# Squares of the first unit split by part over ScalarE and VectorE, one square of products moved to VectorE in two units, and a longer assumed delay for K~ read back from memory

## The chip, the cores and the metric

The kernel runs on one core of a Trainium2 chip. The metric is the device time of one execution in microseconds (us), given as the median of several runs. The core has five engines that run beside each other and meet at semaphores: TensorE (PE in the profile, with its weight loads apart as PEld), VectorE (DVE), ScalarE (ACT), GpSimd (POOL) and SyncE (SP). Transfers to and from memory go by DMA queues, whose issues stand on SP, POOL or ACT.

## The reference: what is computed

A gated linear attention with a complex decay feeds a two-layer block with a squared ReLU between the layers. Batch 4, 8 heads, sequence 768, head size 48; the block is 384 wide and 2048 deep, over 3072 tokens.

```python
mag = np.sqrt(a_re * a_re + a_im * a_im)
scale = np.minimum(mag, 0.999) / (mag + 1e-06)
a_re_n, a_im_n = (a_re * scale, a_im * scale)
for t in range(S):
    ar, ai = (a_re_n[:, :, t, :, None], a_im_n[:, :, t, :, None])
    new_re = ar * S_re - ai * S_im
    new_im = ar * S_im + ai * S_re
    kv = np.einsum('bhd,bhe->bhde', k[:, :, t], v[:, :, t])
    S_re, S_im = (new_re + kv, new_im)
    y[:, :, t] = np.einsum('bhd,bhde->bhe', q[:, :, t], S_re)
# x = y by tokens, heads side by side: (3072, 384)
h = x @ w_in
r = np.maximum(h, 0.0)
out = (r * r) @ w_out
```

## The kernel before

The work is cut into 8 units: one half sequence (384 steps) of one batch entry each, numbered n = 0 to 7. Within a unit the 8 heads stand in two groups of four, z = 0 and z = 1. Each unit has three parts.

The **chain** makes the running products of the decay. On 128 partitions with three steps each (c = 0, 1, 2) it squares the decays, adds the squares, gets 1/mag by logarithm, exponential and a correction step, limits the magnitude, multiplies the three steps of a partition (the "inner" products), takes the reciprocal of the squared magnitude of these products, and turns the last product of each partition by TensorE so that a scan along the free dimension can finish the products over all 384 steps.

```python
def square(z):
    u["fa", z] = wk.tile([C, 2, HH, W, D], F32, name=f"fa{z}", tag=f"fa{z}")
    u["fb", z] = wk.tile([C, 2, HH, W, D], F32, name=f"fb{z}", tag=f"fb{z}")
    act.activation(out=whole(u["fa", z]), in_=whole(u["a", z]), func=AF.Square,
                   accum_out=sums[:, n, z:z + 1])      # sums: watched for overflow

def add_squares(z):
    f0, f1, g0, _ = parts(z)
    dve.tensor_tensor(out=g0, in0=f0, in1=f1, op=ALU.add)
# ...
D1, A1 = dve_cost(NEL), act_cost(NEL)                  # NEL = 4 * 3 * 48 = 576
one("sq", "ACT", act_cost(2 * NEL) + 90,
    lambda z: [("ld", n, "a", z, 1), ("ap", n - 1, z), ("carry", n - 1, 0)], square)
one("m2", "DVE", D1, lambda z: [("sq",)], add_squares)
one("ln", "ACT", A1, ...)                              # log of mag squared
one("ex", "ACT", A1, ...)                              # 1/mag
one("s2", "ACT", A1, ...)                              # its square
one("r1", "DVE", D1, ...); one("r2", "DVE", D1, ...)   # correction step
one("n1", "ACT", A1, ...); one("n2", "ACT", A1, ...)
one("l1", "DVE", D1, ...); one("l2", "DVE", dve_cost(2 * NEL), ...)   # limit
# "in10" ... "in23": the inner products, 16 instructions of VectorE per unit
one("me", "ACT", A1 + 90, lambda z: [("r2",)], lambda z: measure(2 + z, parts(z)[3]))
one("e1", "ACT", ..., lambda z: ends(z, 0))            # copy the last products
one("iq", "ACT", act_cost(2 * NEL), lambda z: [(f"in{W - 1}3",)],
    lambda z: act.activation(out=whole(u["fa", z]), in_=whole(u["a", z]),
                             func=AF.Square))
one("ia", "DVE", D1, lambda z: [("iq",)], add_squares)
one("il", "ACT", A1, ...); one("ie", "ACT", A1, ...)
one("i1", "DVE", D1, ...); one("i2", "DVE", D1, ...)
# ("tot", n, j) on PE turns the last products; ("et", n, j) copies them from PSUM into e
# the scan: 11 products on VectorE over e ("times", "plus")
```

The **pair steps** take two heads at a time: transposes of Q and K ("tq"), scores ("sa"), the outer products of K and V ("kv"), the mix into y ("mix"), and y's way into xT by DMA. "kv" reads K~ in another order of its rows than the chain leaves it in, so K~ goes through memory: "rows" writes it and "KC" reads it back, both as DMA on GpSimd's queue.

```python
for name, lag, deps in (
        ("rows", 4800 if whole_z else 3800, keys + [...]),
        ("KC", 5200 if whole_z else 4200,        # whole_z: units 2 to 7
         [("rows", n, z, pairs[0])] + [...])):
    add((name, n, z, pairs[0]), "POOL", 750, deps,
        lambda z=z, i=pairs[0], name=name: rows(z, i, name == "KC"),
        rank=-100, lag=lag)
```

The **dense steps** are the two layers: 48 products "h" (128x384) and 48 products "o" per unit.

All steps are first collected with an engine, a cost, a lag, a rank and what they depend on. A list scheduler in the kernel's source (`lay_out`) then places them on a model clock, and the steps are emitted in that order. So costs and lags in the source are assumptions: they change no duration on the chip, only the fixed order of the instructions on each engine.

```python
def step(key, engine, cost, rank, deps, fn, lag=None, bank=None, until=None):
    steps[key] = (engine, cost, LAG.get(engine, 0) if lag is None else lag, rank,
                  deps, fn, bank, until)
# lay_out: done[key] = t + cost + lag; a step is ready when all it depends on is done;
# among those ready at nearly the same time the lowest rank is taken
for _, key in lay_out():
    emit(steps[key][5])
```

## Time and profile before

Three runs took 755.68, 757.92 and 759.61 us. The profiled execution took 756.12 us by the same measure and spans 754.3 us in the trace.

| engine | busy us | share of the span | instructions |
|---|---|---|---|
| TensorE, matmul | 708.0 | 94% | 3578 |
| TensorE, weight load | 475.0 | 63% | 3578 |
| VectorE | 504.6 | 67% | 1200 |
| ScalarE | 412.6 | 55% | 764 |
| GpSimd | 113.7 | 15% | 165 |

| stretch, us | PE busy | DVE busy | ACT busy | what runs |
|---|---|---|---|---|
| 0 to 24.4 | 0.00 | 14.95 | 12.11 | unit 0's chain up to the inner products |
| 24.4 to 34.7 | 3.80 | 7.49 | 8.79 | squares of the products, reciprocal, first scan step |
| 34.7 to 47.5 | 10.43 | 12.18 | 8.67 | the scan; PE runs filler products |
| 60 to 85 | 23.16 | 23.36 | 12.54 | pair steps of unit 0, weights converted |
| 85 to 112 | 26.82 | 25.73 | 23.87 | first layer of unit 0 |
| 112 to 145 | 33.00 | 30.09 | 16.02 | second layer of unit 0, chain of unit 1 |
| 300 to 400 | 98.24 | 79.24 | 68.17 | units 3 and 4 |
| 400 to 500 | 99.15 | 87.30 | 68.25 | units 5 and 6 |

How to read it: the second table shows the stages apart, because the shares over the whole span hide that in the first 24.4 us PE does nothing at all, while in the middle it is busy nearly all the time. "Busy" counts instructions in execution; a row of the timeline gives the start, the duration, the engine, the source line, the operation with output and input, and in brackets the idle time just before it with what ended it.

### The profile page before, as it was taken

What the parts mean: (1) busy time and instruction counts of PE and PEld (TensorE: products, weight loads), DVE (VectorE), ACT (ScalarE), POOL (GpSimd) and SP (SyncE); (2) the same over time, 40 slices, a digit from 0 to 9 for tenths busy, and PEclk for the clock granted to TensorE, in tenths of its full rate; (3) what the DMA queues carried; (4) which work ended last, traced back from release to release, by engine and by line L of the source; (5) the groups of instructions that cost most, each with busy time, mean ns of one, the idle gap of its engine ahead of it and who ended that gap; (6) DMA issues with size and microseconds to landing.
All of it is one profiled execution on the core that took longest, in us unless ns stands there. A gap on an engine that the chain in (4) does not pass through costs nothing.

```text
span 754.3 us, 10015 instructions
## 1 busy us (share of the span) xinstructions
PE 708.0 (94%) x3578; PEld 475.0 (63%) x3578; DVE 504.6 (67%) x1200; ACT 412.6 (55%) x764; POOL 113.7 (15%) x165
## 2 busy tenths in 40 slices
PE   0389899999999999999999999999999999999996
PEld 0258555686667766766776676677677555555553
DVE  5899998977698897679689889958953561000000
ACT  6646495256938657762886578776155204402500
POOL 5003100052013013011301211210021430000000
PEclk9999999999999999999999999999999999999999
DMA  9617760054026114222602432340050990000000
GB/s 283 177 41 214 246 211 12 21 168 127 1 72 197 29 50 165 82 59 83 187 18 48 168 111 48 117 152 24 24 189 8 302 306 34 0 23 10 1 10 24
DMA packets 39195, 76.25 MB, mean 101 GB/s; under 512 B 10880, under 2 KB 25312, under 8 KB 39136
## 3 DMA queue, kind: packets, MB, share of 16 engines
q0 software_dynamic: 14336, 53.88, 22.8%
q1 hardware_dynamic: 24672, 21.49, 9.3%
q8 instruction: 30, 0.49, 0.3%
q14 instruction: 29, 0.24, 0.1%
q10 hardware_dynamic: 128, 0.15, 0.1%
HBM read 56.62 MB, written 14.16 MB: 94 GB/s over the span
## 4 chain that ended last, share of the span: by engine, by line
PE 85%; DMA 5%; DVE 4%; ACT 2%; issue 1%; POOL 0%; ACTq 0%; POOLq 0%
PE o L1428 33%; PE h L1411 30%; PE sa L1280 5%; PE tq L1267 4%; DMA KC<-rows 4%; PE kv L1294 4%; PE P L1151 2%; PE ypair L1319 2%; PE ypair L1324 1%; DMA xT<-yt 1%; PE tot L953 1%; PE bk L953 1%; PE y L1319 1%; PE y L1324 1%; PE busy L1068 1%
## 5 line engine op out<-in xcount | busy, mean ns | idle before, releaser
L1411 PE MATMUL h<-xT,w 128*128 128x384 f32 x768 | 256.7, 487 | 2.2 <-DMA xT<-yt 2.2
L1428 PE MATMUL o<-w,g 128*128 128x384 f32 x768 | 255.3, 487 | 0.0
L1411 PEld LDWEIGHTS h<-xT,w 128*128 128x128 f32 x768 | 142.3, 190 | 93.6 <-issue 3.7
L1428 PEld LDWEIGHTS o<-w,g 128*128 128x128 f32 x768 | 142.9, 190 | 91.9 <-issue 0.2
L1418 ACT ACTIVATE g<-h 128x384 f32<-128x384 f32 x128 | 62.3, 487 | 90.2 <-PE h L1411 89.9
L1272 ACT COPY QKT<-tq 96x512 f32<-96x512 f32 x96 | 77.0, 867 | 36.2 <-PE tq L1267 35.7
L1433 ACT COPY ot<-o 128x384 f32<-128x384 f32 x24 | 11.5, 478 | 116.6 <-PE o L1428 116.5
L1421 ACT ACTIVATE g<-g 128x384 f32<-128x384 f32 x128 | 65.8, 522 | 2.9
L1267 PE MATMUL tq<-ident,QK 128*96 128x128 f32 x384 | 51.7, 273 | 1.2 <-DVE QK L1157 1.2
L1280 PE MATMUL sa<-QKT 96*128 96x128 f32 x384 | 52.4, 279 | 0.1
L1280 PEld LDWEIGHTS sa<-QKT 96*128 96x128 f32 x384 | 48.1, 192 | 6.1 <-issue 0.8
L1018 DVE TENSOR_TENSOR fa<-e 128x192 f32<-128x192 f32 (+4 forms) x144 | 48.1, 371 | 5.3 <-ACT e L989 3.1
L1267 PEld LDWEIGHTS tq<-ident,QK 128*96 128x96 f32 x384 | 42.9, 126 | 11.7 <-issue 7.7
L1286 DVE TENSOR_TENSOR A<-sa,mask 128x384 f32<-128x384 f32 x64 | 35.1, 553 | 21.0 <-PE sa L1280 20.0
L824 DVE TENSOR_TENSOR fb<-fa 128x576 f32<-128x576 f32 x32 | 24.1, 755 | 28.7 <-ACT fa L923 17.9
L953 PE MATMUL tot<-ident,last 128*128 128x128 f32 x72 | 12.5, 296 | 30.3 <-ACT last L878 24.4
L832 DVE SCALAR_TENSOR_TENSOR fb<-fb 128x576 f32<-128x576 f32 x48 | 35.1, 753 | 7.6 <-ACT fb L827 7.1
L827 ACT ACTIVATE fa<-fb 128x576 f32<-128x576 f32 x48 | 30.9, 676 | 13.6 <-DVE fb L824 11.3
L1025 DVE TENSOR_TENSOR e<-fa,fa 128x96 f32<-128x96 f32 (+6 forms) x160 | 35.7, 283 | 2.6
L1168 POOL DMA_DIRECT2D rows<-QK x20 | 12.6, 629 | 163.9 <-DVE QK L1157 162.9
L1294 PE MATMUL kv<-v,KC 128*96 128x48 f32 x320 | 31.4, 246 | 3.5 <-DMA KC<-rows 3.5
L1294 PEld LDWEIGHTS kv<-v,KC 128*96 128x96 f32 x320 | 30.4, 165 | 6.8 <-ACT g L1418 2.3
(122 smaller groups left out, 854.2 us busy)
## 6 DMA issues: line engine op xcount, KB each, us to landing
rows<-QK POOLq DMA_DIRECT2D x12, 576.0 KB, 3.6
raw<-in_moe_w_in_dram POOLq DMA_DIRECT2D x16, 384.0 KB, 7.8
look<-in_moe_w_in_dram POOLq DMA_DIRECT2D x16, 384.0 KB, 4.7
look<-in_moe_w_out_dram POOLq DMA_DIRECT2D x16, 384.0 KB, 4.5
raw<-in_moe_w_out_dram SPq DMA_DIRECT2D x13, 384.0 KB, 5.0
out_dram<-ot SPq DMA_DIRECT2D x24, 192.0 KB, 1.9
v<-in_v_dram POOLq DMA_DIRECT2D x18, 192.0 KB, 4.4
a<-in_a_re_dram POOLq DMA_DIRECT2D x12, 288.0 KB, 3.4
```

The source lines that it names most:

```text
L832: dve.scalar_tensor_tensor(out=f[dst[-1]], in0=f[2] if i == 0 else f[dst[0]], scalar=scalar, in1=f[by], op0=ALU.add if i else ALU.mult, op ...
L1018: dve.tensor_tensor(out=t, in0=x(e), in1=y(e)[:, j].unsqueeze(1) .to_broadcast(shape), op=ALU.mult)
L1025: dve.tensor_tensor(out=dst(u["e"])[:, r], in0=temp(0)[:, r], in1=temp(1)[:, 1 - r], op=ALU.add if r else ALU.subtract)
L1267: nc.tensor.transpose(ps[:, 2 * j + h], src, ident)
L1272: act.copy(out=u["T", i].rearrange("r z (p c) -> r c z p", c=W)[:, c], in_=u["tq", i, c])
L1280: nc.tensor.matmul(sa[:, j], lhsT=T[:, 2 + h, ts(j, C)], rhs=T[:, h, ts(j, C)], start=True, stop=True)
L1286: dve.tensor_tensor(out=u["A", i][:, h], in0=u["sa", i, h], in1=mask3, op=ALU.mult)
L1294: nc.tensor.matmul(ps[:, j, h], lhsT=u["KC", hh // HH][:, j, hh % HH], rhs=u["v"][:, j, hh], start=True, stop=True)
L1411: nc.tensor.matmul(u["h", f], lhsT=w1[:, f, m], rhs=u["xT"][:, m], start=(m == 0), stop=(m == NM - 1))
L1418: act.activation(out=t, in_=u["h", f], func=AF.Relu)
L1421: act.activation(out=u["g", f], in_=u["g", f], func=AF.Square)
L1428: nc.tensor.matmul(u["o", c], lhsT=u["g", f][:, ts(c, C)], rhs=w2[:, f], start=(f == 0), stop=(f == NF - 1))
```

## The change

The change has four parts and a small fifth. Its aim is a shorter way to TensorE's first work, and an order of TensorE's instructions that does not meet the transfer of K~ before it has landed.

1. Unit 0's squares of the decays: the square over both parts (1152 elements a partition, with a sum over the elements) is split. ScalarE squares the real part (576) as soon as that part has landed, VectorE squares the imaginary part by a multiplication with itself. The sum for the overflow watch is taken later, by a copy of the added squares with a sum ("ms"). The assumed lags of the four loads are set anew.
2. Units 0 and 1, group z = 1: the square of the inner products ("iq") is done by VectorE instead of ScalarE.
3. The assumed lag of "KC" in units 2 to 7 goes from 5200 to 7000.
4. `minus`, a negated identity, is made by ScalarE later, as a step of its own before the products that use it.
5. `LATER`, a rank, goes from 150 to 155, so that the ranks of the few postponed steps keep their place behind the steps that were added.

```diff
-    act.mul(out=minus, in_=ident, mul=-1.0)
...
-                        lag=(3300 + 2500 * z if name == "a" else 8000) if n == 0 else 6000)
+                        lag=(3100 + 1100 * z + 300 * j if name == "a" else 8000)
+                        if n == 0 else 6000)
...
+            elif r == 0:
+                act.activation(out=parts(z)[0], in_=flat(u["a", z][:, 0]), func=AF.Square)
+            else:
+                a = flat(u["a", z][:, 1])
+                dve.tensor_tensor(out=parts(z)[1], in0=a, in1=a, op=ALU.mult)
...
+        if n == 0:
+            one("sq", "ACT", A1, lambda z: [("ld", n, "a", z, 0)], lambda z: square(z, 0))
+            one("sqi", "DVE", D1, lambda z: [("ld", n, "a", z, 1), ("sq",)],
+                lambda z: square(z, 1))
+            one("ms", "ACT", A1 + 90, lambda z: [("m2",), ("me",)],
+                lambda z: measure(z, parts(z)[2], AF.Copy), rank=900)
+            add(("minus",), "ACT", 190, [("me", 0, 1)],
+                lambda: act.mul(out=minus, in_=ident, mul=-1.0), rank=910)
+        else:
+            one("sq", "ACT", act_cost(2 * NEL) + 90, ..., square)
+        one("m2", "DVE", D1, lambda z: [("sq",), ("sqi",)], add_squares)
...
-        one("iq", "ACT", act_cost(2 * NEL), lambda z: [(f"in{W - 1}3",)], ...)
-        one("ia", "DVE", D1, lambda z: [("iq",)], add_squares)
+        def square_products(z):
+            a, fa = whole(u["a", z]), whole(u["fa", z])
+            if n < 2 and z:
+                dve.tensor_tensor(out=fa, in0=a, in1=a, op=ALU.mult)
+            else:
+                act.activation(out=fa, in_=a, func=AF.Square)
+        both(lambda z: add(("iq", n, z), *(("DVE", dve_cost(2 * NEL)) if n < 2 and z else
+                                           ("ACT", act_cost(2 * NEL))),
+                           [(f"in{W - 1}3", n, z)], lambda: square_products(z)))
+        one("ia", "DVE", D1, lambda z: [("iq",), ("ms",)], add_squares)
...
-        LATER = 150
+        LATER = 155
...
-                        ("KC", 5200 if whole_z else 4200,
+                        ("KC", 7000 if whole_z else 4200,
```

Because the order is made from the assumed costs and lags, the change also moves instructions that the diff does not name. TensorE's order is the same up to the pair steps of unit 3. From there the first "kv" of units 3, 4, 6 and 7 stands later or behind other products, and from there to the last units the order differs in many places; VectorE's order differs in the two squares, in the first scan steps of units 0 and 1, and in the later units where it follows TensorE's.

## The prediction

> **What bounds the kernel now.** I read the engine totals and the slices of the page first, then TensorE's waits, then the timeline where the two meet.

> ```profile
> PE 708.0 (94%) x3578; PEld 475.0 (63%) x3578; DVE 504.6 (67%) x1200; ACT 412.6 (55%) x764; POOL 113.7 (15%) x165
> ...
> PE   0389899999999999999999999999999999999996
> ```

> Each digit is a fortieth of the span, 18.9 us. TensorE is idle in the first and part of the second and third slice and then close to full. So there are two ways to shorten the kernel without taking work from TensorE: let it start earlier, and take away its waits later. The waits are few:

> ```profile
> PE tot L953 <- ACT last L878: 24.4, 1, 24.4
> PE tot L953 <- ACT last L880: 5.9, 2, 4.9
> PE kv L1294 <- DMA KC<-rows: 3.5, 4, 1.8
> PE bk L953 <- DVE e L1025: 2.2, 1, 2.2
> PE h L1411 <- DMA xT<-yt: 2.2, 2, 1.4
> ```

> The columns are total us, times, longest. The first, second and fourth line are unit 0's chain; the third is K~ read back. In the chain the last to be ready is nearly always VectorE (12.18 of 12.80 us busy from 34.7 to 47.5 us), so I look for VectorE's gaps before that:

> ```profile
> 9.40 0.76 DVE L824 TENSOR_TENSOR fb<-fa 128x576 f32<-128x576 f32 x1 [2.61 <-ACT fa L819]
> ...
> 12.34 0.76 DVE L832 SCALAR_TENSOR_TENSOR fb<-fb 128x576 f32<-128x576 f32 x1 [0.61 <-ACT fb L827]
> ...
> 25.81 0.76 DVE L824 TENSOR_TENSOR fb<-fa 128x576 f32<-128x576 f32 x1 [1.79 <-ACT fa L923]
> 27.71 0.76 DVE L824 TENSOR_TENSOR fb<-fa 128x576 f32<-128x576 f32 x1 [1.14 <-ACT fa L923]
> ```

> From 12.34 us to 24.0 us VectorE has no gap; then it waits 1.79 and 1.14 us for ScalarE's two squares of the products (1.16 us each). These gaps are what the second part of the change aims at. The waits for K~ in units 3, 4 and 6:

> ```profile
> 297.56 1.53 PE L1294 MATMUL kv<-v,KC 128*96 128x48 f32 x16 [0.36 <-DMA KC<-rows]
> 368.46 1.19 PE L1294 MATMUL kv<-v,KC 128*96 128x48 f32 x12 [1.76 <-DMA KC<-rows]
> 492.60 2.21 PE L1294 MATMUL kv<-v,KC 128*96 128x48 f32 x24 [0.85 <-DMA KC<-rows]
> ```

> Together 2.97 us; the fourth wait, 0.53 us, is in unit 0, whose lag is not changed.

> [...] 758 and 1354 ns. The new squares on VectorE are tensor_tensors of these sizes, so I take 0.76 and 1.36 us. [...] every ScalarE row of the first 30 us starts after the row that stands before it in the order. [...] For K~ of a whole group (576 KB) [...] here it is 5.7 us in the median and 8.0 at most, and the measurement decides. So the source's new 7000 is the more honest one.

> **The change, part by part.**

> *Unit 0's first squares.* Landing times in the DMA view (issue plus time to landing): real and imaginary part of group 0 at 0.81 + 3.0 = 3.8 and 1.30 + 3.3 = 4.6 us; of group 1 at 1.84 + 5.0 = 6.8 and 2.39 + 5.4 = 7.8. Removed from ScalarE: two squares of 1.15 and two accumulator reads of 0.19 us. Added: two squares of 0.68 us (as the other 576-element activations), and on VectorE two of 0.76 us. ScalarE's new order is square 0, square 1, logarithm 0. Square 1 waits for 6.8 and ends near 7.6, so logarithm 0 starts near 7.6, where it now starts at 6.82[...]. What counts is when VectorE can run without gaps, at the second group's correction step, now 12.34. After: imaginary squares on VectorE at 4.7 and 7.85, sums of squares at 5.5 and 8.6, ready by 9.4. ScalarE from 7.6 does three activations per group at 0.72 us each, six in all: the last starts at 7.6 + 5 x 0.72 = 11.2 and ends at 11.9. So VectorE's unbroken stretch begins near 11.9 instead of 12.34. **Gain 0.4 to 0.5 us.** The new sums ("ms", 0.67 + 0.19 us each) fall in ScalarE's idle 7.86 us before 23.79, and so does `minus` (0.29): free.

> *Unit 0's squares of products.* Now VectorE loses 1.79 + 1.14 + 0.1 = 3.0 us in gaps between 24.0 and 29.0. After: VectorE squares group 1 itself as soon as the inner products end (1.3 us start to start), then adds group 1's squares (0.7); in that time ScalarE, which copies the last products (0.93) and squares group 0 (1.16) from 0.3 us before the same moment, is done, and group 0's sum follows without a gap. The copies of the turned products from PSUM (two, 0.93 us) come next on ScalarE and end 2.6 us after the inner products; VectorE is then 2.7 us on. So almost no gap: 3.0 - 1.3 = **1.7 us gain**. That the order puts four more scan instructions before the reciprocal's correction steps only shifts work within a stretch in which VectorE is full.

> With 0.45 from the front this is 2.1 us earlier for the scan's end at 45.8 us, and for all that follows: from there to 80 us VectorE (23.36 of 25 us) and TensorE (23.16 of 25) feed each other, and the transfers in it start from results, so they move along. The weights land long before they are used.

> *Unit 1's squares of products.* The same edit, but the gaps there are 1.79 and 0.30 us, and after the sums the scan waits for the turned products: TensorE gets to turn them only at 127.83, between second-layer products. After: square 125.75, sums at 127.05 and 127.75, ended 128.5; the copies from PSUM on ScalarE still end near 129.3, and the scan starts at 129.35, where it starts now (129.34). Gaps removed 2.09, work added 1.3, new gap 0.8: **0.0 us**.

> *K~'s lag.* From the first transposes of the unit (which start when "rows" is issued) to the first "kv", TensorE's order holds, with "h" of three 1.94 us, "o" of four 2.58, transposes of eight 0.87, scores of six 1.48:

> | unit | landed after | TensorE work ahead, before | after |
> |---|---|---|---|
> | 3 | 11.0 us | 10.65 | 13.3 |
> | 4 | 12.2 us | 10.55 | 13.3 |
> | 6 | 11.3 us | 10.65 | 11.8 |

> (For unit 3: 3 x 0.87 + 3 x 1.94 + 1.48 + 0.74 = 10.65; the new order puts 0.74 + 1.94 more ahead.) All three waits are covered, unit 6 with 0.5 us to spare. TensorE is otherwise full there, so what it doesn't wait is gained: up to 2.97, I take **2.7 us**.

> *What is given back.* From unit 3 on TensorE's order is another one, and the mix after a late "kv" now has 1.94 us between them in which VectorE adds up to six small states (0.28 us each): enough, but with less room. I put 0.5 us for new small waits.

> Sum: 2.1 + 0.0 + 2.7 - 0.5 = 4.3 us; 757.92 - 4.3 = **753.6 us**, 0.6% less.

> **The rivals.**

> *The K~ wait only changes its name.* ScalarE is busy 12.14 of 12.50 us in the 12.5 us before unit 4's "kv", with copies of the transposes and the squared ReLU of "h". If the products put ahead of "kv" are "h", each brings 1.0 us of ScalarE work and PSUM room must come free: TensorE could wait for ScalarE instead. For it speaks that number; against it that the page shows no TensorE wait for ScalarE behind unit 0, and that 1.94 us of "h" brings only 1.0 of ScalarE. It would give back 1.5 to 3 us: 755 to 757.

> *The head's gain is lost at a transfer.* TensorE waits 0.53 us for K~ and 1.44 us for xT at the end of unit 0's pair steps; if a transfer there were held by traffic that does not move along (weights at 178 GB/s in 60 to 85), the 2.1 us would shrink. Against it: those transfers are issued when their data is ready. It would leave 1 us of the head: 754.7.

> *VectorE pays for unit 1.* From 85 to 112 us it is busy 25.73 of 27, and 1.3 us of work is added in unit 1; if the turned products come earlier than I think the gap of 0.8 is not there (gain 0.8), if VectorE is late the reverse: 753 to 755.

> **Range and chances.** The three runs before spread over 3.9 us, so a median may be off by 1 to 1.5 us; the reordered units I put at 1.5 to 2 us. That gives 750.0 to 757.2 for 8 in 10. A gain of over 2% (15 us) would need about all of TensorE's waits after the first one (5.9 + 3.5 + 2.2 + 2.2 and 2.0 in smaller ones = 15.8 us); a loss of over 2% would need new waits of 15 us in an order that only moves one group of products by 2 to 4 us. Faster by over 2%: 0.01, within 2%: 0.97, slower by over 2%: 0.02.

> **What would show it.** In the changed profile: logarithm 0 starting near 7.6 us; TensorE's first wait near 23.9 instead of 24.4; VectorE's gaps after 24 us under 0.3 us in sum; the scan's end near 43.7; first-layer products of unit 0 resuming near 83.1 instead of 85.19; no waits of "kv" for K~ in units 3, 4 and 6. The prediction is wrong if the scan's end moves by less than 1.5 us, if the 2.1 us are gone by 85 us, or if TensorE's waits behind 185 us stay at 3 us under another name.

## The result, and the profile after

The changed kernel took **749.55 us** in the median (748.03 to 750.53, four runs), the kernel before 757.66 (755.68 to 759.61, four runs): a ratio of 0.9891, 95% interval 0.9859 to 0.9923. The prediction was 753.6 with a range of 750.0 to 757.2, so the time fell below the range. In three later series, on three chips, the ratios were 0.9907 (0.988 to 0.9935), 0.9926 (0.9906 to 0.9946) and 0.9898 (0.9873 to 0.9923). In differences of means these are 6.9, 5.9 and 7.1 us; the working had summed to 4.3.

The page of the changed kernel, engine totals and TensorE's slices (now 18.7 us each):

```profile
PE 704.8 (94%) x3578; PEld 473.7 (63%) x3578; DVE 508.7 (68%) x1204; ACT 412.0 (55%) x764; POOL 114.8 (15%) x165
...
PE   0379899999999999999999999999999999999996
```

TensorE does the same 3578 products in 3.2 us less busy time, which is a first hint that something other than waits has changed: equal products took less time. VectorE has its four added instructions.

TensorE's waits in the changed kernel (total us, times, longest):

```profile
PE tot L979 <- ACT last L886: 23.9, 1, 23.9
PE tot L979 <- ACT last L888: 5.6, 2, 5.4
PE kv L1320 <- DMA KC<-rows: 2.2, 1, 2.2
PE h L1437 <- DMA xT<-yt: 1.8, 2, 1.3
PE tq L1293 <- DVE QK L1183: 1.7, 1, 1.7
PE bk L979 <- DVE e L1051: 1.7, 1, 1.7
```

The first wait is 0.5 us shorter. "kv" waits for K~ once instead of four times, and the one that is left is in unit 0 and has grown from 0.53 to 2.24 us. From 200 us to 740 us the list of waits is empty. Line numbers are higher by 26 in this part of the source.

VectorE's timeline in the changed kernel, at the same places as in the prediction:

```profile
5.83 0.76 DVE L832 TENSOR_TENSOR fb<-fa 128x576 f32<-128x576 f32 x1
...
9.80 0.76 DVE L840 SCALAR_TENSOR_TENSOR fb<-fb 128x576 f32<-128x576 f32 x1 [0.20 <-ACT fb L835]
...
11.81 0.76 DVE L840 SCALAR_TENSOR_TENSOR fb<-fb 128x576 f32<-128x576 f32 x1 [0.45 <-ACT fb L835]
...
23.52 1.36 DVE L943 TENSOR_TENSOR fa<-a 128x1152 f32<-128x1152 f32 x1
24.98 1.43 DVE L832 TENSOR_TENSOR fb<-fa 128x576 f32<-128x576 f32 x2
26.52 0.92 DVE L1044 TENSOR_TENSOR fa<-e 128x192 f32<-128x192 f32 x2
```

A row without a bracket had no idle time before it. The second group's correction step starts at 11.81 instead of 12.34 us; from there VectorE runs through, its own square of the products (1.36 us) included, and the gaps of 1.79 and 1.14 us are gone. On ScalarE the first logarithm starts where the working put it, near 7.6:

```profile
7.08 0.68 ACT L825 ACTIVATE fa<-a 128x576 f32<-128x576 f32 x1 [2.23 <-DMA a<-in_a_re_dram]
7.67 0.67 ACT L835 ACTIVATE fa<-fb 128x576 f32<-128x576 f32 x1
```

Its input, the added squares of group 0 (the first row of VectorE's timeline), is ready at 6.59 us. The logarithm still starts 1.1 us later, behind group 1's square, which stands ahead of it in ScalarE's order and waits 2.23 us for its load.

The scan's last instruction (the second of L1051 over 279 elements, L1025 before) ends at 43.50 instead of 45.78 us. TensorE's timeline in the changed kernel where the head of the kernel (all that stands ahead of unit 1's first layer, up to about 185 us) comes to its transfers:

```profile
75.92 1.22 PE L1320 MATMUL kv<-v,KC 128*96 128x48 f32 x12 [2.24 <-DMA KC<-rows]
...
83.75 27.33 PE L1437 MATMUL h<-xT,w 128*128 128x384 f32 x84 [1.31 <-DMA xT<-yt]
```

Of the 2.3 us gained at the scan's end 1.44 us are left where the first layer resumes (83.75 against 85.19): the longer wait for K~ took the rest in this execution.

| point, us | before | after | gain so far |
|---|---|---|---|
| scan's last instruction ends | 45.78 | 43.50 | 2.28 |
| unit 0's first layer resumes | 85.19 | 83.75 | 1.44 |
| unit 1's first layer resumes | 184.78 | 182.98 | 1.80 |
| last product of TensorE ends | 748.22 | 742.77 | 5.45 |

The last two rows differ by 563.44 us before and 559.79 after. So this pair of executions puts 3.65 us into the part behind 185 us and 1.8 into the head. The medians of the later series are farther apart than that, and what is missing had to be looked for in executions, not in one profile.

### The profile page after: what moved, and what is told of

Its sections match the earlier page's. It is cut to its first block, busy times and chain, and to the rows that moved or that the text cites. A ratio compares the mean times of both kernels' runs of the same rounds, so it can differ in the third digit from the quotient of the medians.

```text
span 748.8 us, 10017 instructions
## 1 busy us (share of the span) xinstructions
PE 704.8 (94%) x3578; PEld 473.7 (63%) x3578; DVE 508.7 (68%) x1204; ACT 412.0 (55%) x764; POOL 114.8 (15%) x165
## 4 chain that ended last, share of the span: by engine, by line
PE 89%; DMA 3%; SPq 3%; DVE 2%; issue 1%; ACT 1%; POOL 0%; ACTq 0%; POOLq 0%
PE o L1454 33%; PE h L1437 32%; PE sa L1306 6%; PE tq L1293 5%; PE kv L1320 3%; SPq L783 2%; PE ypair L1345 2%; PE P L1177 2%; PE ypair L1350 1%; DMA xT<-yt 1%; PE tot L979 1%; DMA v<-in_v_dram 1%; PE bk L979 1%; DMA KC<-rows 1%; PE y L1345 1%
## 5 line engine op out<-in xcount | busy, mean ns | idle before, releaser
L979 PE MATMUL tot<-ident,last 128*128 128x128 f32 x72 | 12.3, 296 | 29.5 <-ACT last L886 23.9
L832 DVE TENSOR_TENSOR fb<-fa 128x576 f32<-128x576 f32 x32 | 24.0, 755 | 20.1 <-ACT fa L945 15.4
L1051 DVE TENSOR_TENSOR e<-fa,fa 128x96 f32<-128x96 f32 (+6 forms) x160 | 35.4, 283 | 2.6
L783 POOL DMA_DIRECT2D v<-in_v_dram x18 | 15.9, 888 | 115.3 <-PE y L1350 75.8
```

Of the source, the lines that this page charges most:

```text
L1051: dve.tensor_tensor(out=dst(u["e"])[:, r], in0=temp(0)[:, r], in1=temp(1)[:, 1 - r], op=ALU.add if r else ALU.subtract)
```

## The theories, and the experiments

**The working's own theory**: the gain is the sum of its steps, each wait being worth its length. **Rivals**: a part of the sum is mis-sized (the K~ step worth more, or the head worth less because a transfer eats it); or, called **theory D** in the expectations, a TensorE wait of 1 to 2 us has a price beside its length, because TensorE runs at half its clock for some microseconds afterwards (3.4 us in the kernel before, from 46.72 to 50.13 us). Each expectation says in its own words what else it sets against what.

The differences below are of means, against the kernel before run in the same series on the same chip; the medians of the kernel before were 754.69, 754.71, 755.26 and 755.54 in the four series. The ratio, with its 95% interval, is an estimate of its own and not the quotient of these means; the two differ by up to 0.8 us (fetch_late: 4.9 us by the means, 4.1 by the ratio). Where the text says "either way" it means twice the standard error of a difference of means.

| kernel | median us | runs | less than before, us | ratio (95%) |
|---|---|---|---|---|
| after_again | 748.35 | 6 | 6.85 | 0.9907 (0.988 to 0.9935) |
| kc_only | 752.35 | 22 | 2.67 | 0.996 (0.9947 to 0.9974) |
| no_kc | 750.47 | 13 | 3.96 | 0.9941 (0.9918 to 0.9963) |
| iq_only | 752.41 | 22 | 2.47 | 0.9972 (0.9956 to 0.9989) |
| fill_all | 755.14 | 14 | 0.03 | 0.9997 (0.9984 to 1.0011) |
| fewer_fill | 749.83 | 6 | 4.95 | 0.9941 (0.9924 to 0.9958) |
| fetch_late | 750.57 | 6 | 4.93 | 0.9945 (0.9924 to 0.9966) |
| iq_u0 | 748.98 | 6 | 5.75 | 0.9933 (0.9914 to 0.9952) |
| after_third | 749.45 | 6 | 5.89 | 0.9926 (0.9906 to 0.9946) |
| late_fill | 749.76 | 6 | 5.91 | 0.9931 (0.9912 to 0.9951) |
| fill_head | 754.34 | 14 | 1.09 | 0.9988 (0.9969 to 1.0006) |
| no_iq | 751.68 | 22 | 3.68 | 0.9956 (0.9944 to 0.9968) |
| more_before | 753.16 | 22 | 1.99 | 0.9972 (0.9958 to 0.9986) |
| fewer_before | 753.83 | 22 | 1.39 | 0.998 (0.9964 to 0.9996) |
| more_after | 748.68 | 6 | 6.75 | 0.9905 (0.988 to 0.9931) |
| after_fourth | 748.79 | 6 | 7.06 | 0.9898 (0.9873 to 0.9923) |

### The change taken apart

**after_again** is the changed kernel without an edit, in the first series.

> The changed kernel once more, to see which part of the 8.1 us between the medians is there on one chip in alternation. Theory A (the two profiled executions are typical): 5 to 6 us faster than before, as their spans differ by 5.5 us, and TensorE again without a wait for K~ in units 3 to 7. Theory B (the kernel before usually waits longer for K~ than in its profiled execution): 7 to 9 us faster. Theory C (the TensorE clock falls to one half around 47 to 50 us in the kernel before and in some executions costs more than the 0.8 us seen): also 7 to 9, with a full clock here at 45 to 50 us.

It gave 6.85 us. The gain of over 6 us is no accident of the first four runs, though the 8.1 us of those was: the kernel before, at 757.66 there, has medians of 754.7 to 755.5 in every later series.

**kc_only** is the kernel before with K~'s lag alone. TensorE's order is then that of the changed kernel.

```diff
-                        ("KC", 5200 if whole_z else 4200,
+                        ("KC", 7000 if whole_z else 4200,
```

> The kernel before with nothing but K~'s assumed lag at 7000; TensorE's order is then exactly that of the changed kernel. Theory A: 3.0 to 3.8 us faster (the three waits of 2.97 us, and 0.7 us less in TensorE's rows of units 3 to 7). Theory B: 5 to 6.5 us faster, since more than the profiled waits goes. Theory C: 3 to 3.8, since the clock in the head is not touched. In all: no wait of kv for K~ behind 185 us, scan's end at 45.8 as before.

It gave 2.67 us (0.8 either way), and TensorE's waits from 60 to 700 us are these:

```profile
PE h L1411 <- DMA xT<-yt: 1.6, 2, 1.1
PE kv L1294 <- DMA KC<-rows: 0.4, 1, 0.4
```

Only unit 0's wait for K~ is left; no wait came in place of the three that went. In this profile TensorE needs 559.79 us (184.16 to 743.95) from unit 1's first layer to its end, as in the changed kernel to the hundredth. The K~ step and the "nothing is given back" are both read from this number: 563.44 - 559.79 = 3.65 us, of which 2.97 are the waits.

**no_kc** is the changed kernel with K~'s lag back at 5200.

```diff
-                        ("KC", 7000 if whole_z else 4200,
+                        ("KC", 5200 if whole_z else 4200,
```

> The changed kernel with K~'s lag back at 5200: only the head's parts remain. Theory A: 1.8 us faster than before (1.44 at 85 us and 0.33 more at 185 us in the profiled pair). Theory B: 1.5 to 2.5. Theory C: 4 to 5 us. The waits for K~ in units 3, 4 and 6 return, 2 to 4 us in sum.

It gave 3.96 us (1.5 either way). With kc_only the two halves sum to 6.63, where the whole gave 6.85 in the same series: within this scatter they add. The head's part can be had more sharply from the same series: after_again and kc_only have the same order on TensorE, product by product, and differ only by the edits of the head, and after_again's mean is **4.2 us** lower (0.6 either way). That is twice the 2.1 of the working. So the surplus is in the head, and the profile of this run shows what else a wait can do. Its TensorE timeline in unit 4:

```profile
366.06 1.19 PE L1320 MATMUL kv<-v,KC 128*96 128x48 f32 x12 [1.31 <-ACT g L1444]
...
367.82 1.78 PE L1320 MATMUL kv<-v,KC 128*96 128x48 f32 x12
...
370.81 4.05 PE L1437 MATMUL h<-xT,w 128*128 128x384 f32 x6
```

The kernel before at the same place, after a wait of 1.76 us:

```profile
371.94 2.10 PE L1411 MATMUL h<-xT,w 128*128 128x384 f32 x6
```

The same six products take 4.05 instead of 2.10 us. The windows of no_kc (length, then busy time of PE, PEld, DVE, ACT and POOL, then the granted TensorE clock, DMA share and GB/s) name the reason in the third column from the end:

```profile
366.00:368.00 2.00, 1.94 (x21) 1.97 (x22) 0.64 (x3) 1.78 (x3) 0.37 (x1) 1.00 0.03 12
368.00:370.00 2.00, 2.00 (x15) 2.00 (x14) 1.57 (x5) 0.69 (x2) 2.00 (x4) 0.53 0.48 55
370.00:372.00 2.00, 2.00 (x7) 1.48 (x7) 1.38 (x4) 1.36 (x2) 1.38 (x2) 0.50 0.98 382
372.00:374.00 2.00, 2.00 (x4) 1.01 (x3) 1.93 (x4) 0.00 (x0) 0.00 (x0) 0.50 1.00 313
374.00:376.00 2.00, 2.00 (x24) 1.22 (x24) 0.53 (x1) 1.08 (x3) 0.00 (x0) 0.76 0.40 134
```

The clock falls to half at 368.13 us, 2.1 us after the end of a wait of 1.31 us, and stays there until 374.95, for 6.8 us. That is theory D's mechanism, and "busy" hides it: PE is busy 1.94 to 2.00 of 2.00 us in these windows.

**iq_only** is the kernel before with the square of the products of group 1 on VectorE, units 0 and 1.

```diff
-        one("iq", "ACT", act_cost(2 * NEL), ...)
+            if n < 2 and z:
+                dve.tensor_tensor(out=fa, in0=a, in1=a, op=ALU.mult)
+            else:
+                act.activation(out=fa, in_=a, func=AF.Square)
```

> The kernel before with only the squares of products of group 1 on VectorE in units 0 and 1; TensorE's order is that of before. By the prediction's step the scan's end moves from 45.8 to 44.1 us (1.7) and unit 1 gives 0. Theory A: of the 1.7 about 0.9 is left at 85 us, because K~ of unit 0's last pair is delayed by transfers of weights that don't move along: 0.7 to 1.2 us faster. Theory C: if the shorter idle time of TensorE ahead of 45 us keeps the clock full, 2 to 4 us faster.

It gave 2.47 us (1.0 either way); the scan ends at 44.26, against 44.1 by the working (45.8 less 1.7).

**no_iq** is the changed kernel with that edit undone.

> The changed kernel with the squares of products on ScalarE in both units and groups, as before: what the split of the first squares is worth beside K~'s lag. By the prediction's step the scan's end comes at 45.3 us (0.45 earlier than before, 1.7 to 2.3 later than in the changed kernel); by the sum of the other runs (iq alone gave 2.1 to 2.5 us) 750.5 to 751.5 us.

It gave 3.68 us. With 5.89 of after_third in the same series, the squares of the products are worth 2.2 us there; less kc_only's 2.67, the first squares are worth about 1.0, with an uncertainty as large as itself (1.1 either way). VectorE's two gaps are back, as its timeline shows:

```profile
25.30 0.76 DVE L832 TENSOR_TENSOR fb<-fa 128x576 f32<-128x576 f32 x1 [1.79 <-ACT fa L941]
27.20 0.76 DVE L832 TENSOR_TENSOR fb<-fa 128x576 f32<-128x576 f32 x1 [1.14 <-ACT fa L941]
```

They begin 0.5 us earlier than in the kernel before, which is the first squares' step; the scan ends at 45.28.

**iq_u0** is the changed kernel with the square of the products on VectorE in unit 0 alone.

```diff
-            if n < 2 and z:
+            if n < 1 and z:
```

> The changed kernel with the square of products on VectorE in unit 0 alone; unit 1 as before. The prediction's step said that unit 1 gives 0.0 us: then this is within 0.3 us of the changed kernel (748.3). If VectorE's two gaps in unit 1 (2.1 us before) were a real loss, 0.5 to 0.8 us slower.

It gave 5.75 us (1.5 either way), where the changed kernel gave 5.9 to 7.1 in the other series: unit 1's part is worth nothing that can be seen in six runs.

**after_third** and **after_fourth** are the changed kernel again, as yardsticks of the third and fourth series.

> The changed kernel a third time, as the reference for the other three on this chip. 748 to 749.5 us, 5.5 to 7 us under before. If the extra gain over the prediction comes from the stage ahead of unit 1's first layer (kernels with the new order took 559.8 us from there to TensorE's end in every profile), that stage ends near 181 to 182 us here and near 185 in before.

> The changed kernel again, as the yardstick for the three others: 5.5 to 6.5 us less than the kernel before in the mean (it was 6.8 and 5.9), the scan's end between 42.8 and 43.5 us.

One profile is one execution; the chain's two steps are read better from all eighteen. TensorE's first product "tot" comes when the inner products of group 0 are ready, so its start shows the first squares; the time from there to the scan's end shows the squares of the products.

| quantity and kernels | profiles | mean us | lowest and highest |
|---|---|---|---|
| start of "tot", first squares as before | 7 | 24.59 | 24.40, 25.09 |
| start of "tot", first squares split | 11 | 23.58 | 23.15, 24.15 |
| "tot" to the scan's end, squares of products on ScalarE | 7 | 21.34 | 21.32, 21.37 |
| "tot" to the scan's end, group 1's on VectorE | 11 | 19.59 | 19.53, 19.63 |

So the squares of the products move the scan's end by 1.75 us, and the first squares by 1.0 us, twice what the working had; in the first pair of profiles it was 0.5. The difference lies mostly in the landing of group 1's real part, for which the new order holds the first logarithm back: from its issue it took 4.1 to 5.9 us in the eighteen profiles, 4.7 in the mean, and 5.0 in the one execution that the working used. ScalarE's square of it starts at 7.08 us in the first profile of the changed kernel and at 6.5 in the mean of the eleven. Together the scan's end comes 2.75 us earlier in the mean, and of the head's 4.2 us some 1.4 (0.7 either way) are not in the chain.

### The clock

In the profile of each kernel TensorE's wait ahead of the scan's end and the clock afterwards stand so:

| wait ahead of the scan's end | profiles | clock at half afterwards |
|---|---|---|
| 2.0 to 2.2 us | before, kc_only, no_iq, after_again, after_fourth; fill_all | in the first five; not in fill_all |
| 3.5 and 5.3 us | fewer_fill, fewer_before | in both |
| 1.7 us or less, or none | after, iq_only, no_kc, iq_u0, after_third, fetch_late, fill_head, late_fill, more_before, more_after | in none |

The change shortens this wait (to 1.2 to 2.0 us in the four profiles of the changed kernel, of which two still have the half clock), and so it can take away the half clock as well as the wait; that gain stands in no list of waits.

Why do waits of the same length end differently? The clock's records answer this in part. In eight profiles with two or more changes of the clock (before, no_kc, no_iq, fewer_fill, fewer_before, fill_head, after_third and after_fourth) these lie 3.41 us or a multiple of it apart: in the kernel before at 46.72, 50.13 and 753.28 us (1 and 206 steps of 3.413), in fill_head at 79.86, 83.26, 492.86, 496.28 and 752.28 us (1, 120, 1 and 75 steps). Counted on from a change, these steps cut an execution into windows of 3.41 us, which lie elsewhere in each execution (one ends at 46.72 us in before, at 46.36 in no_iq). What followed a wait went, in the cases below, with whether it fell into one window or was cut by the end of one. Two executions of the changed kernel at unit 0's wait for K~, in such windows (columns as above):

```profile
71.35:74.77 3.42, 2.29 (x26) 1.84 (x20) 3.42 (x9) 2.17 (x4) 0.00 (x0) 1.00 0.72 208
74.77:78.18 3.41, 2.27 (x32) 2.12 (x32) 1.03 (x5) 0.57 (x1) 0.00 (x0) 1.00 0.13 33
```

That is the first profile; its wait of 2.24 us ends at 75.92, so it is cut in two, each window has about 1.1 us of idle time, and the clock stays full. And after_third:

```profile
71.67:75.08 3.41, 1.97 (x21) 1.52 (x15) 3.41 (x9) 1.82 (x4) 0.00 (x0) 1.00 0.79 241
75.08:78.49 3.41, 3.41 (x26) 3.30 (x28) 1.18 (x6) 0.55 (x1) 0.00 (x0) 0.50 0.07 17
```

Its wait is shorter, 1.42 us, but lies in one window, and the clock is at half for the next two, until 81.91. From the scan's end to unit 1's first layer this execution takes 141.13 us, the three other profiles of the same kernel 138.29 to 139.48. Likewise the wait of 1.76 us in unit 4 of the kernel before is cut by the end of a window at 367.57, and fill_all's of 2.12 us at 44.54; the clock stays full behind both. One limit for the idle time does not come out: from 38 to 52 us 1.95 us in one window and more were followed by half clock in seven of seven cases and 1.70 us or less in none, but behind 360 us 0.91 us was enough (fill_head at 489.45), and at 80.32 us 1.85 us was not (late_fill).

The next experiments change only the number of filler products (the "busy" products on the identity, each of two instructions, whose results nothing uses; four of them take 2.4 us in more_before), or fill the waits for K~ the same way.

**fill_all** is the kernel before with two more fillers ahead of the scan's end, and with products on the identity in front of the first "kv" of units 3, 4 and 6 that last about as long as the waits there (and one in unit 0).

```diff
+            for _ in range({(0, 3): 1, (3, 0): 1, (4, 0): 3, (6, 0): 2}.get((n, i), 0)):
+                nc.tensor.matmul(..., lhsT=ident[:, 0:R], rhs=..., start=True, stop=True)
...
-                    [("scan", n, 3 + j // 2, "plus", 1), ("busy", n, j - 1)], busy,
+                    [("scan", n, 3 + j // 2, "plus", 1), ("busy", n, j - 1)],
+                    lambda j=j: busy(2 if n == 0 and j == 8 else 0),
```

> The kernel before, in which TensorE has more to do where it waits: two more filler products (0.81 us each) after the fillers of unit 0's scan, and one, one, three and two products of 128x288 (0.49 us each) ahead of the kv that waits for K~ in units 0, 3, 4 and 6. Nothing starts earlier, TensorE's work grows by 5 us. Theory D (every wait of TensorE of 1 to 2 us can halve its clock for one or two stretches of some 3.4 us after it; this is what the kernel before pays beside the waits themselves): 1.5 to 2.7 us faster than before, mean clock up from 0.994 to 0.997 or more, and the slow tail of the runs (757 to 759) gone. Theory A (only the waits count): 0 to 1 us slower.

A miss for theory D as it was put: the mean granted clock rose from 0.9939 to 0.9984, and the time did not move. TensorE's timeline in unit 4 shows why it could not move there:

```profile
366.97 1.62 PE L1294 MATMUL kv<-ident 128*96 128x288 f32 x6
368.42 1.14 PE L1301 MATMUL kv<-v,KC 128*96 128x48 f32 x12
```

"kv" starts at 368.42, in the kernel before at 368.46. The filler took exactly the place of the wait, in which it costs nothing; but it is of fixed length and the wait is not (in fewer_before's profile all waits for K~ sum to 0.9 us, in the kernel before's to 3.5), and where the wait is shorter the filler would be paid. That this is what used up the gain is argued, not shown.

**fewer_fill** is the changed kernel without four of unit 0's fillers in the last steps of the scan.

```diff
-                    [("scan", n, 3 + j // 2, "plus", 1), ("busy", n, j - 1)], busy,
+                    [("scan", n, 3 + j // 2, "plus", 1), ("busy", n, j - 1)],
+                    (lambda: None) if n == 0 and 5 <= j < 9 else busy,
```

> The changed kernel with four of unit 0's fillers left out (3.3 us of work that nothing uses), so that TensorE idles about 5 us ahead of the scan's end. Theory D: the clock is at one half in nearly every execution behind 43 us, the first products P take 0.69 to 0.85 us instead of 0.41, and the run is 0.5 to 2 us slower than the changed kernel. Theory A: the same time as the changed kernel (748.3).

It gave 4.95 us, 0.8 less than iq_u0 in the same series, which is within the scatter (1.6 either way) and so neither shows nor excludes the loss that theory D expected; the wait grew to 3.46 us and the clock fell as expected.

**fill_head** is the kernel before with four more fillers ahead of the scan's end (the edit of fill_all with 4 for 2, without its first half), and two products on the identity ahead of unit 0's first transposes.

> The kernel before with the same six filler products in the head and nothing else. Theory D: P at 0.41 us and the mean clock up by 0.002; 0.5 to 1.5 us faster than before. Theory A: no difference, or 0.2 slower.

It gave 1.09 us (1.0 either way), with an interval of the ratio that includes 1. The two products ahead of the transposes take 1.45 us (four instructions), and TensorE still waits 0.30 us for VectorE after them: in this profile they delay nothing.

**more_before** is the clean form: the kernel before with the four fillers ahead of the scan's end and nothing else.

```diff
-                    [("scan", n, 3 + j // 2, "plus", 1), ("busy", n, j - 1)], busy,
+                    [("scan", n, 3 + j // 2, "plus", 1), ("busy", n, j - 1)],
+                    lambda j=j: busy(4 if n == 0 and j == 8 else 0),
```

> The kernel before with four more filler products (about 0.34 us each) right ahead of TensorE's wait for the scan's end; nothing else. Theory D (that wait of 2.2 us is followed by 4 us of TensorE at half clock in most executions, which costs the head about 1 us): the wait falls to about 0.8 us, P follows at full clock (0.75 us for two), and the time falls by 0.6 to 1.2 us against the kernel before. Rival (the clock costs nothing here, the head's steps were only mis-sized): 0.0 +- 0.3 us; if the fillers overrun the chain, slower by up to 0.5.

It gave 1.99 us (0.9 either way; interval of the ratio 0.9958 to 0.9986), with four products more and no step of the chain moved: the scan ends at 45.77, before at 45.78. TensorE's timeline in the kernel before:

```profile
45.48 0.97 PE L953 MATMUL bk<-ident,e 128*128 128x128 f32 x6 [2.21 <-DVE e L1025]
...
47.54 1.33 PE L1151 MATMUL P<-fa,ident 128*128 128x288 f32 x2 [0.20 <-DVE fa L1138]
...
52.23 1.05 PE L1267 MATMUL tq<-ident,QK 128*96 128x128 f32 x8 [1.21 <-DVE QK L1157]
```

and in more_before:

```profile
45.47 0.97 PE L953 MATMUL bk<-ident,e 128*128 128x128 f32 x6
...
47.53 0.75 PE L1153 MATMUL P<-fa,ident 128*128 128x288 f32 x2 [0.45 <-DVE fa L1140]
...
51.42 1.05 PE L1269 MATMUL tq<-ident,QK 128*96 128x128 f32 x8 [1.68 <-DVE QK L1159]
```

The four fillers took 2.4 us, more than the expectation gave them, and left no wait. "bk" and "P" start at the same time in both. But two products of "P" take 0.75 instead of 1.33 us, VectorE gets its input earlier, and the transposes start 0.81 us earlier. In this pair nothing of it is left where unit 0's first layer resumes, at 85.41 us (85.19 in the kernel before): the wait for K~ ahead of it is 1.84 us, in the kernel before 0.53. The profiled execution took 755.88 us, and more_before's median is 753.16; where the 2.0 us lie in the faster executions no profile shows. The mean granted clock of all its runs fits: 0.9974 against 0.9941, and 0.0033 of 754 us is an estimate of 2.5 us of full clock.

**fewer_before** is the kernel before with fewer_fill's edit.

> The kernel before without its fillers of steps 5 to 8, so that the wait ahead of the scan's end grows from 2.2 to about 4 us. Theory D: the kernel before halves its clock there anyway in most executions, so little is added: +0.0 to +0.6 us against the kernel before, P at 1.17 to 1.33 us for two. Rival (the clock costs nothing): 0.0. If a longer wait also lengthens the half-clock stretch: over +0.6.

The sign was missed: 1.39 us *less*. Its TensorE timeline:

```profile
45.42 1.54 PE L953 MATMUL bk<-ident,e 128*128 128x128 f32 x6 [5.33 <-DVE e L1025]
...
48.04 1.13 PE L1152 MATMUL P<-fa,ident 128*128 128x288 f32 x2
49.00 0.65 PE L1152 MATMUL P<-fb,minus 128*128 128x288 f32 x2
...
52.05 1.05 PE L1268 MATMUL tq<-ident,QK 128*96 128x128 f32 x8 [1.43 <-DVE QK L1158]
```

Here the clock fell at 42.17 us, in the middle of the wait, and was back at 49.00, 3.6 us after work resumed; in the kernel before it was at half from 46.72 to 50.13, for 3.4 us, all behind the wait. So the work that runs at half clock is about the same in both, though the wait is 3.1 us longer. The transposes start 0.18 us earlier in this profile; the rest of the 1.4 is open. It is not the clock's: the mean granted clock of all runs is 0.9938, of the kernel before 0.9941. This weakens what more_before showed. Two opposite edits of the same wait both made the kernel faster, and their gains differ by no more than the scatter (0.6 us, 0.9 either way), so a reason that they have in common and that no run names is not excluded.

**more_after** is the changed kernel with more_before's edit.

> The changed kernel with the same four fillers. Theory D: its wait is 1.2 to 2.0 us and mostly followed by full clock, so little is left to gain: -0.3 to 0.0 us against the changed kernel (749.4 in the last comparison). Rival: 0.0. If the fillers overrun the chain: up to +0.5.

It gave 6.75 us, and after_fourth 7.06 (748.68 and 748.79 in the median): no difference that six runs each can show, as expected where the wait was mostly short enough already.

This makes a comparison with the wait ahead of the scan's end filled in *both* kernels: 753.71 less 748.95 in the means is **4.8 us**, 0.9 either way. That fits the working's 4.3, and as well the 5.4 that the scan's end in all profiles (2.75) and kc_only (2.67) give, so it does not decide between them. With the fillers as they were, the difference is 5.9 to 7.1.

### Two versions that were to be faster

**fetch_late** is the changed kernel with three late weight loads put behind unit 0's last K~ transfer in GpSimd's order.

```diff
+    moved = [("fetch", i) for i in range(FIRST, NF)]
+    order = [key for key in order if key not in moved]
+    at = order.index(("KC", 0, 1, NP - 1)) + 1
+    order[at:at] = moved
```

> The changed kernel with GpSimd's order changed at one place: three loads of weights (384 KB each) that stood before and behind the last read of K~ in unit 0 are issued after it. If the wait of TensorE for that K~ (2.24 us in the first profile of the changed kernel, 0.39 in the second) comes from these loads, it is under 0.3 us here, K~ lands in under 5 us, and the kernel is 0.5 to 2 us faster than the changed one: 746.5 to 748. If K~ is held by the transfers of xT and rows, nothing changes.

**late_fill** is fetch_late with fill_head's fillers.

> The version to beat both: the changed kernel, the three loads of weights issued after K~ of unit 0's last pair, four more filler products ahead of the scan's end and two of 96x384 ahead of unit 0's first transposes, where TensorE waits 1 to 2 us each. Theory D (waits cost again through the clock): mean clock 0.998 or more, no run over 749.5, median 747 to 748. If the clock in the head is of no weight: the same as the changed kernel.

In fetch_late's profile the last wait for K~ is gone and unit 1's first layer resumes at 180.54 us, 2.4 earlier than in the changed kernel's first profile. But its median is 750.57: three of the six runs stood near 752, at a clock of 0.993, 0.993 and 0.997 (the others 0.998 or 0.999). late_fill has 749.76 with a narrow spread (749.38 to 750.6), and a new wait: TensorE's waits for xT sum to 3.0 us instead of 1.8. Neither beats the changed kernel, and neither does any other kernel here. Why those three runs took longer is open.

## Why the prediction was wrong, point by point

**First squares.** Right in the first profile: the logarithm at 7.67 (near 7.6 in the working), VectorE's unbroken stretch from 11.81 (near 11.9), the first wait 23.9 (near 23.9). Too small in the mean of the profiles: 1.0 us where 0.45 was put down, because the landing of group 1's real part, on which the step hangs, was taken from one execution. That the first profile met the working was luck. VectorE's squares of 576 elements took the 0.76 us that were put down, those of 1152 the 1.36.

**Squares of products, unit 0.** Right: the gaps are gone, and all profiles give 1.75 us where the working had 1.7. The scan's end, 43.7 in the working, came at 42.8 to 43.5 in the four profiles of the changed kernel; the difference is the first squares'.

**Unit 1.** Right as far as iq_u0 can tell: nothing.

**K~'s lag, and what is given back.** kc_only measures both together: 2.67 us (0.8 either way), where 2.7 less 0.5 were put down. The three waits are gone, and nothing was given back in the profiles: the new order has no wait at all behind 200 us, and 559.79 us from unit 1's first layer to the end is its full occupation, the same in eleven profiles to 0.01 us. VectorE's small states kept up.

**The head's gain.** This is the step that failed: "With 0.45 from the front this is 2.1 us earlier for the scan's end at 45.8 us, and for all that follows". The head gave 4.2 us (after_again against kc_only). The first half of the sentence is too small by the first squares: 2.75 us at the scan's end. The second half, that all that follows moves by the same time, leaves out 1.4 us (0.7 either way). What it leaves out can be the clock: the change shortens the wait ahead of the scan's end, 2.21 us, to 1.2 to 2.0, and with it goes, in part of the executions, a stretch at half clock. For this speak more_before, 2.0 us in a kernel where only that wait was filled, and the mean granted clock, 0.9983 in after_again against 0.9954 in kc_only (an estimate of 2.2 us of full clock in 750). Against it speaks fewer_before, 1.4 us faster with more of that wait and no better clock. So the clock as the cause of these 1.4 us is argued, not shown.

**The rival "the head's gain is lost at a transfer"** is true of single executions: unit 0's wait for K~ was 2.24 us in the first profile of the changed kernel, 0.39 in after_again's, 1.0 in after_fourth's. In the first pair of profiles 0.84 of the 2.28 us are gone by unit 0's first layer; the means do not show such a loss. **"The K~ wait only changes its name"** fell by kc_only, but no_kc shows that it was no idle thought: with the lag at 5200 that profile has a wait of 1.31 us put down to ScalarE in unit 4.

**The start value.** The 757.92 us from which the 4.3 were taken came from three runs; the later medians are 2.4 to 3.2 us lower. That error goes the same way as the head's: from 755 the same sum would have given 750.7, and 748.4 to 749.5 was measured in those series. The prediction allowed 1 to 1.5 us for it. Of the 4.0 us between 753.6 and 749.55 this is the larger part, an error of the start and not of the mechanism; the head's missing 2.1 us is the mechanism's.

**Left open**: how much idle time in one window brings the clock down; why fewer_before is faster; where more_before's 2.0 us lie. The correlation of time with the mean granted clock over the first three series of the kernel before is -0.78 (104 runs), but a low clock comes with long waits, so it can't be read as the clock's cost alone: fill_all has the high clock and not the time.

## What to carry to other kernels

Take the landing of a transfer from several executions before an order is built on it: here one execution made a step of 1.0 us look like 0.5. Look at the granted clock as well as at the waits, in windows of the step in which it changes (3.41 us here), because "busy" counts slow products as work (2.00 of 2.00 us at a clock of 0.50 in no_kc): a wait of 1.42 us inside one window was followed by 6.8 us at half clock, one of 2.24 us that two windows share by none. Filling a wait with products that nobody needs is worth a trial and no rule: it gained 2.0 us in more_before, 1.1 in fill_head (1.0 either way) and nothing in fill_all and more_after, and leaving fillers out gained 1.4 in fewer_before. And before explaining a gain below 1%, measure the start value in more than three runs.
